# A convolution and two dense layers on one core: weights read in longer runs and with a stride, and another order of casts, loads and taps at the start

## The chip, the core and the metric

The kernel runs on one core of one Trainium2 chip. The metric is the device time of one execution, in microseconds (us); lower is better. The device time is some 1.7 us more than the span in the trace.

## The reference

x has 8 sequences of 4096 rows with 192 channels. A causal convolution of 7 taps runs along the sequence; the 192 channels are 8 heads of 24, and a head's taps are a softmax of 7 weights. Then each row goes through two dense layers, 192 to 2048 with a leaky ReLU and 2048 to 192.

```python
w = exp(weight - max); w = w / sum(w)                      # (8 heads, 7 taps)
out = np.einsum('hk,bskhg->bshg', w, x_unf)                # causal, 7 taps
h = out.reshape(B * S, D) @ w_in                           # 32768 x 192 @ 192 x 2048
g = np.maximum(0.01 * h, h)
return g @ w_out                                           # 2048 x 192
```

## The kernel before

Rows come in blocks of 512 for a pair of sequences. The first five blocks are worked in halves of 256 (ten half-blocks), the other 27 whole. VectorE does the taps of the convolution (`yt` from `xt`, three chunks of 64 channels for each of the two sequences, seven taps a chunk). TensorE does the hidden layer (`mm1`, from `yt` and `w_in` into PSUM tile `ph`), ScalarE evicts it with the leaky ReLU into `g`, and TensorE does the second layer (`po` from `g` and `w_out`) some blocks behind. Later blocks of x are loaded by casting DMAs that GpSimd issues (`load_x`) and transposed by DMA.

The first two blocks can't wait for that. They come in four "halves" q = 0 to 3, loaded in fp32, cast by an engine, transposed on TensorE and copied out of PSUM by VectorE:

```python
    def load_first(q, after=None):
        t = stage_pool.tile([128, 2, HS, D], FP32, name="x_nat")
        for e in range(2):
            ins = nc.sync.dma_start(out=t[:, e, :, :], in_=x[e, q * HT : (q + 1) * HT, :]...)
            # [cut: with `after`, the load waits for that instruction]

    def cast_first(q, e, copy):          # fp32 -> bf16, by VectorE or ScalarE
        copy(out=x_bf[q // 2][...], in_=x_nat[q][...])

    # [cut] transpose_first(q): 12 transposes on TensorE into PSUM; evac_first(q): two copies to xt
    make_identity(nc, ident)                                         # GpSimd
    nc.vector.tensor_add(ident2, ident[:, 0:CH], ident[:, CH:128])
    sel = const_pool.tile([H, NCH, 2, CH], BF16, name="sel")         # GpSimd: memset, two selects
    # [cut]
    w_in = const_pool.tile([128, NCH, F], BF16)                      # four quarters
    for fs in (slice(0, F // 2), slice(F // 2, F)):
        for e in range(2):
            nc.gpsimd.dma_start(out=w_in[e * CH : (e + 1) * CH, :, fs], in_=...)
    nc.gpsimd.dma_start(out=w_out, in_=moe_w_out.rearrange("(c p) d -> p c d", p=128))
    # [cut] softmax of the taps, beginning with nc.vector.tensor_reduce(out=nmax, ...)
```

In the loop over the groups, half-block 0 carries the special work (`u` counts the eight hidden steps):

```python
                act = mm1(grp, u)
                if i == 0 and u == 3:
                    for job in pe_ahead: job()       # one chunk of half 1's taps on TensorE
                if i == 0 and u in (0, 6):
                    load_first(2 + u // 6, act)
                if i == 1 and u in (2, 3):
                    cast_first(3, u - 2, nc.scalar.copy)
            # [cut]
            if i == 0 and j == 3:
                evac_y(nc.vector.tensor_scalar_mul)
                for e in range(2):
                    cast_first(2, e, nc.vector.tensor_copy)
                transpose_first(2)
                evac_first(2, nc.vector.tensor_copy, nc.vector.tensor_copy)
```

Of the kernel before, what the change touches and what calls it, by code (L numbers as in the profile page):

```python
# [14 lines left out]
def kernel(  # L15
# [28 lines left out]
    NHALF = 5  # L44
    NPEC = 2
# [59 lines left out]
    def load_first(q, after=None):  # L105
        t = stage_pool.tile([128, 2, HS, D], FP32, name="x_nat")
        for e in range(2):
            ins = nc.sync.dma_start(
                out=t[:, e, :, :],
                in_=x[e, q * HT : (q + 1) * HT, :].rearrange("(c p) d -> p c d", p=128),  # L110
            )
            if after is not None and e == 0:
                tc.add_manual_dep(
                    ins.ins, after.ins.name,
                    mybir.DependencyInfo(
                        mybir.DependencyClass.Sync, mybir.DependencyReason.DATA
                    ),
                    reason="leave the DMA engines to the weights",
                )
        x_nat[q] = t  # L120

    def cast_first(q, e, copy):
        if q % 2 == 0 and e == 0:
            x_bf[q // 2] = xb_pool.tile([128, NCH, SUB, 2, CH], BF16, name="x_bf")
        h = q % 2
        copy(  # L126
            out=x_bf[q // 2][:, :, h * HS : (h + 1) * HS, e, :],
            in_=x_nat[q][:, e, :, :].rearrange("p s (c k) -> p c s k", c=NCH),
        )
# [3 lines left out]
    def transpose_first(q):  # L133
        ts = [
            psum_o.tile([128, HS, NCH, CH], BF16, name=f"ptr{i}", tag="po") for i in range(2)
        ]
        for s in range(HS):
            for c in range(NCH):
                for i in range(2):
                    ps = slice(i * CH, (i + 1) * CH)  # L140
                    nc.tensor.transpose(  # L141
                        out=ts[i][:, s, c, :],
                        in_=x_bf[q // 2][ps, c, (q % 2) * HS + s, :, :].rearrange(
                            "p e k -> p (e k)"
                        ),
                        identity=ident[ps, ps],
                    )
        ptr[q] = ts

    def evac_first(q, *copies):  # L150
        dst = xt[0][:, :, HALO + q * HT : HALO + (q + 1) * HT].rearrange(
            "p c (s i k) -> p i s c k", s=HS, i=2
        )
        for i, t in enumerate(ptr.pop(q)):
            copies[i](out=dst[:, i], in_=t)  # L155
# [60 lines left out]
    nc.vector.memset(junk, 0.0)  # L216
    ident = const_pool.tile([128, 128], BF16)
# [4 lines left out]

    sel = const_pool.tile([H, NCH, 2, CH], BF16, name="sel")
    nc.gpsimd.memset(sel, 1.0)  # L224
    for sign, off in ((1, 0), (-1, GRP - 1)):
        nc.gpsimd.affine_select(  # L226
            out=sel, in_=sel, compare_op=mybir.AluOpType.is_ge, fill=0.0,
            base=off, channel_multiplier=-sign * GRP,
            pattern=[[sign * CH, NCH], [0, 2], [sign, CH]],
        )  # L230


    w_in = const_pool.tile([128, NCH, F], BF16)
    for fs in (slice(0, F // 2), slice(F // 2, F)):
        for e in range(2):
            nc.gpsimd.dma_start(  # L236
                out=w_in[e * CH : (e + 1) * CH, :, fs],
                in_=moe_w_in[:, fs].rearrange("(c p) f -> p c f", p=CH),
            )
    w_out = const_pool.tile([128, NFC, D], BF16)  # L240
    nc.gpsimd.dma_start(out=w_out, in_=moe_w_out.rearrange("(c p) d -> p c d", p=128))
# [4 lines left out]
    def warm(n):  # L246
        for _ in range(n):
            nc.tensor.matmul(  # L248
                out=wa[:, 0, 0:HT], lhsT=zero[:, 0:128], rhs=zero, start=True, stop=True
            )  # L250
# [20 lines left out]
    warm(9)  # L271
    wps = psum_h.tile([128, 2, ST], FP32, name="wps", tag="ph")
# [3 lines left out]
    def select(out, parts):  # L276
        for c in range(NCH):
            nc.tensor.matmul(
                out=out[:, c], lhsT=sel[:, c, :, :].rearrange("h e k -> h (e k)"),
                rhs=w9p[:, parts, :], start=True, stop=True,  # L280
            )
# [4 lines left out]
    warm(5)  # L286
# [44 lines left out]

    for n, job in enumerate(conv_jobs(groups[0], range(NPEC, NCH))):
        if n in (4, 5):
            cast_first(1, n - 4, nc.vector.tensor_copy)
        job()
    for c in range(NPEC):
        pe_jobs, evac_y = pe_conv_jobs(groups[0], c)
        for job in pe_jobs:
            job()
        evac_y(act_scale)  # L340
        if c == 0:
            warm(2)
    transpose_first(1)
    evac_first(1, nc.vector.tensor_copy, nc.vector.tensor_copy)


# [7 lines left out]
    SINGLE = LAST - 2  # L354

    def mm1(grp, u):
        blk, t0, T = grp
        y = yt[blk]
        nf = ST // T
        ph = psum_h.tile([128, 2, ST], FP32, name="ph", tag="ph")  # L360
        for i in range(nf):
            f = nf * u + i
            for c in range(NCH):
                for e in range(2):
                    ps = slice(e * CH, (e + 1) * CH)
                    nc.tensor.matmul(  # L366
                        out=ph[:, e, i * T : (i + 1) * T],
                        lhsT=w_in[ps, c, f * 128 : (f + 1) * 128],
                        rhs=y[ps, c, t0 : t0 + T],
                        start=(c == 0),  # L370
                        stop=(c == NCH - 1),
                    )
        act = nc.scalar.activation(  # L373
            out=g[blk][:, nf * u : nf * (u + 1), :, t0 : t0 + T],
            in_=ph.rearrange("p e (i t) -> p i e t", i=nf),
            func=mybir.ActivationFunctionType.Prelu, alpha=0.01,
        )
        return act
# [74 lines left out]
    pjunk = const_pool.tile([1, 1], BF16)  # L453
    slot, avail = 0, 0
    for i, grp in enumerate(groups):
# [11 lines left out]
        for j in range(steps):  # L467
            for u in range(2 * j, 2 * j + 2):
                act = mm1(grp, u)
                if i == 0 and u == 0:  # L470
                    pe_ahead, evac_y = pe_conv_jobs(groups[1], 0)
                    ahead = conv_jobs(groups[1], range(1, NCH))
                    per = len(ahead)
                if i == 0 and u == 3:
                    for job in pe_ahead:
                        job()
                if i == 0 and u in (0, 6):
                    load_first(2 + u // 6, act)
                if i == 1 and u in (2, 3):
                    cast_first(3, u - 2, nc.scalar.copy)  # L480
# [11 lines left out]
            if i == 0 and j == 3:  # L492
                evac_y(nc.vector.tensor_scalar_mul)
                for e in range(2):
                    cast_first(2, e, nc.vector.tensor_copy)
                transpose_first(2)
                evac_first(2, nc.vector.tensor_copy, nc.vector.tensor_copy)
            if i == 1 and j == 1:

                nc.gpsimd.tensor_copy(out=pjunk, in_=g[0][0:1, NFC - 1, 1, HT - 1 : HT])  # L500
                load_x(2)
# [4 lines left out]
            if i == 1 and j == 1:  # L506
                transpose_first(3)
# [44 lines left out]
```

## Time and profile before

| | before |
|---|---|
| time, median | 694.78 us (694.33 to 695.75, 3 runs); 694.98 with one more run |
| span of the profiled run | 693.2 us |
| TensorE, VectorE, ScalarE busy | 99%, 79%, 74% |
| first hidden step runs through from | 12.71 us |
| VectorE's copies of half 1 begin | 11.55 us |
| VectorE has finished block 5's convolution | 118.72 us |

TensorE's 99% says that little can be won at all: it is idle for 9.1 us of 693.2 (684.1 busy). Where a part of it can be won has to be read from the waits, engine by engine. The prediction below shows TensorE's. The following is VectorE's timeline of the kernel before: the softmax's first operation, then half 1's copies and what follows. Columns of all timelines below: start in us, duration in us, engine, source line, operation, output and input, how many in a row, and in brackets the idle time ahead with what ended it.

```profile
2.18 0.15 DVE L255 TENSOR_REDUCE nmax<-w 8x1 f32<-8x7 f32 x1 [0.57 <-DMA w<-in_weight_dram]
...
11.55 0.61 DVE L155 COPY xt<-ptr 128x384 bf16<-128x384 bf16 x2
...
18.85 0.48 DVE L205 TENSOR_SCALAR yt<-acc,rsum 128x256 bf16<-128x256 f32 x1
20.02 0.42 DVE L126 CAST x_bf<-x_nat 128x384 bf16<-128x384 f32 x1 [0.69 <-DMA x_nat<-in_x_dram]
21.25 0.43 DVE L126 CAST x_bf<-x_nat 128x384 bf16<-128x384 f32 x1 [0.81 <-DMA x_nat<-in_x_dram]
22.12 0.62 DVE L155 COPY xt<-ptr 128x384 bf16<-128x384 bf16 x2 [0.44 <-PE ptr L141]
...
26.10 0.58 DVE L174 TENSOR_SCALAR yt<-xt,wk 128x256 bf16<-128x256 bf16 x1
...
33.58 0.52 DVE L174 TENSOR_SCALAR yt<-xt,wk 128x256 bf16<-128x256 bf16 x1
...
37.14 0.28 DVE L174 TENSOR_SCALAR yt<-xt,wk 128x256 bf16<-128x256 bf16 x1
...
114.03 4.69 DVE L180 SCALAR_TENSOR_TENSOR yt<-xt,wk,yt 128x512 bf16<-128x512 bf16 x6
```

From 18.85 to 22.12 VectorE does no taps: 3.27 us of an eviction (of the chunk whose taps TensorE did), two casts and three waits. And the first tap of a chunk, always the same 128 x 256 operation, takes 0.28 us at 37.14 but 0.58 and 0.52 earlier.

### The profile page before, as it was taken

Reading aid. Unit: us, or ns where it says so; the run is one execution under the profiler, and the core shown is the slowest. Engines: PE = TensorE matmul, PEld = TensorE weight load, DVE = VectorE, ACT = ScalarE, POOL = GpSimd, SP = SyncE. Lnnn points to the kernel's source line nnn. Section 1 sums busy time; section 2 is a strip of 40 time slices with the busy share of each in tenths; the row PEclk is TensorE's granted clock in tenths of the full one; section 3 lists DMA queues with packets and bytes.
Section 4 is the critical chain, followed back from the end, with each engine's and each line's share of the span. In section 5 each row is a group of like instructions: output and inputs, shape, how many; then the busy total and the mean of one; then the engine's idle time right before and its main releaser. Section 6 shows DMA issues by size and latency. Waiting matters only on the chain.

```text
span 693.2 us, 26064 instructions
## 1 busy us (share of the span) xinstructions
PE 684.1 (99%) x11778; PEld 539.5 (78%) x11778; DVE 544.4 (79%) x1005; ACT 516.4 (74%) x577; POOL 139.6 (20%) x195
## 2 busy tenths in 40 slices
PE   7999999999999999999999999999999999999998
PEld 5899998677777777777777777777777777777777
DVE  7899998977878787878877888878777878787812
ACT  6788888977777777777777777777777777777771
POOL 3632201502222102222012222112222012000000
PEclk9999999999999999999999999999999999999999
DMA  9995636935565445565355664455655455222112
GB/s 167 124 102 81 87 67 82 90 73 70 72 88 79 72 77 76 74 82 84 69 81 74 78 82 78 78 70 75 86 82 78 74 75 66 70 60 59 48 36 70
DMA packets 184096, 54.39 MB, mean 78 GB/s; under 512 B 148400, under 2 KB 183216, under 8 KB 183984
## 3 DMA queue, kind: packets, MB, share of 16 engines
q0 software_dynamic: 97936, 14.17, 29.6%
q1 hardware_dynamic: 86048, 38.56, 22.7%
q8 instruction: 92, 1.51, 1.0%
q14 instruction: 20, 0.16, 0.1%
HBM read 29.88 MB, written 25.17 MB: 79 GB/s over the span
## 4 chain that ended last, share of the span: by engine, by line
PE 93%; DMA 3%; DVE 2%; ACT 1%; POOL 0%; issue 0%; SPq 0%; POOLq 0%; DVEq 0%
PE po L392 48%; PE ph L366 45%; DVE yt L180 2%; DMA w_in<-in_moe_w_in_dram 1%; DMA x_nat<-in_x_dram 1%; DMA xt<-x_bf 1%; ACT g L373 0%; POOL sel L226 0%; DVE yt L174 0%; ACT x_bf L126 0%; POOL w_in L236 0%; PE ptr L141 0%; DVE x_bf L126 0%; SPq L447 0%; POOL sel L224 0%
## 5 line engine op out<-in xcount | busy, mean ns | idle before, releaser
L373 ACT ACTIVATE g<-ph 128x1024 bf16<-128x1024 f32 x512 | 496.3, 1021 | 156.4 <-PE ph L366 156.1
L180 DVE SCALAR_TENSOR_TENSOR yt<-xt,wk,yt 128x512 bf16<-128x512 bf16 (+1 forms) x648 | 442.4, 683 | 17.6
L392 PEld LDWEIGHTS <-g 64*128 64x128 bf16 (+1 forms) x8064 | 352.3, 94 | 45.3 <-issue 0.2
L392 PE MATMUL po<-w_out,g 64*128 64x192 bf16 (+1 forms) x8064 | 382.7, 243 | 0.0
L366 PE MATMUL ph<-yt,w_in 64*128 64x512 bf16 (+1 forms) x3552 | 379.3, 347 | 3.1 <-DMA w_in<-in_moe_w_in_dram 1.2
L366 PEld LDWEIGHTS <-w_in 64*128 64x128 bf16 x3552 | 186.4, 94 | 98.6 <-issue 4.9
L77 POOL DMA_DIRECT2D x_bf<-in_x_dram x180 | 133.6, 772 | 422.4 <-DMA xt<-x_bf 420.0
L439 DVE COPY o_sb<-po 128x192 f32<-128x192 f32 x216 | 77.1, 358 | 121.1 <-PE po L392 115.3
L174 DVE TENSOR_SCALAR yt<-xt,wk 128x512 bf16<-128x512 bf16 (+1 forms) x108 | 38.0, 352 | 2.1 <-DMA xt<-x_bf 2.1
L439 ACT COPY o_sb<-po 128x192 f32<-128x192 f32 x40 | 12.8, 320 | 1.9
L248 PE MATMUL warm<-zero 128*128 128x256 bf16 x24 | 5.1, 367 | 1.1 <-DVE junk L216 1.1
L199 PE MATMUL acc<-xt,diag 64*64 64x256 bf16 x84 | 5.2, 270 | 0.5 <-DVE xt L155 0.5
L199 PEld LDWEIGHTS <-diag 64*64 64x64 bf16 x84 | 4.3, 106 | 1.3 <-DVE xt L155 0.8
L303 ACT ACTIVATE diag<-ident,whm 128x64 bf16<-128x64 bf16 x14 | 3.6, 335 | 1.9 <-DVE whm L289 1.9
L248 PEld LDWEIGHTS <-zero 128*128 128x128 bf16 x24 | 2.5, 124 | 2.2 <-DVE junk L216 1.1
L126 DVE CAST x_bf<-x_nat 128x384 bf16<-128x384 f32 x5 | 2.3, 453 | 1.5 <-DMA x_nat<-in_x_dram 1.5
L500 POOL COPY pjunk<-g 1x1 bf16<-1x1 bf16 x1 | 0.2, 178 | 16.1 <-ACT g L373 16.1
L141 PEld LDWEIGHTS <-x_bf 64*128 64x128 bf16 x48 | 1.0, 94 | 2.5 <-ACT x_bf L126 1.9
L141 PE MATMUL ptr<-ident,x_bf 64*128 64x64 bf16 x48 | 1.4, 191 | 1.4 <-ACT x_bf L126 0.9
L236 POOL DMA_DIRECT2D w_in<-in_moe_w_in_dram x4 | 2.6, 660 | 0.0
L155 DVE COPY xt<-ptr 128x384 bf16<-128x384 bf16 x7 | 2.2, 351 | 0.5 <-PE ptr L141 0.4
L253 ACT ACT_TABLE_LOAD x1 | 1.3, 1283 | 0.8 <-PEq L536 0.8
(35 smaller groups left out, 12.9 us busy)
## 6 DMA issues: line engine op xcount, KB each, us to landing
out_dram<-o_sb SPq DMA_DIRECT2D x123, 192.0 KB, 2.1
x_bf<-in_x_dram POOLq DMA_DIRECT2D x180, 64.0 KB, 3.3
x_nat<-in_x_dram SPq DMA_DIRECT2D x8, 192.0 KB, 3.9
w_in<-in_moe_w_in_dram POOLq DMA_DIRECT2D x4, 384.0 KB, 9.7
xt<-x_bf SPq DMA_TRANSPOSE x90, 2.6
out_dram<-o_sb SPq DMA_DIRECT2D x10, 96.0 KB, 1.6
w_out<-in_moe_w_out_dram POOLq DMA_DIRECT2D x1, 768.0 KB, 16.5
w<-in_weight_dram SPq DMA_DIRECT2D x1, 0.2 KB
```

Of the source, the lines that this page charges most:

```text
L77: nc.gpsimd.dma_start(out=t[:, c, :, e, :], in_=src[2 * rp + e, :, :, c * CH : (c + 1) * CH],)
L141: nc.tensor.transpose(out=ts[i][:, s, c, :], in_=x_bf[q // 2][ps, c, (q % 2) * HS + s, :, :].rearrange("p e k -> p (e k)"), identity=ident ...
L174: lambda s=src, d=dst, c=c: nc.vector.tensor_scalar_mul(d, s, wk[:, c, 0:1])
L180: lambda s=src, d=dst, c=c, k=k: nc.vector.scalar_tensor_tensor(out=d, in0=s, scalar=wk[:, c, k : k + 1], in1=d, op0=mybir.AluOpType.mult, ...
L199: lambda k=k, p=p, a=a, e=e, ps=ps: nc.tensor.matmul(out=acc[ps, :T], lhsT=diag[c][ps, p, k, :], rhs=xt[0][ps, c, a : a + T], start=(k == ...
L236: nc.gpsimd.dma_start(out=w_in[e * CH : (e + 1) * CH, :, fs], in_=moe_w_in[:, fs].rearrange("(c p) f -> p c f", p=CH),)
L248: nc.tensor.matmul(out=wa[:, 0, 0:HT], lhsT=zero[:, 0:128], rhs=zero, start=True, stop=True)
L303: nc.scalar.activation(out=diag[c][:, 1, k, :], in_=ident2, func=mybir.ActivationFunctionType.Copy, scale=whm[:, c, 1, k : k + 1],)
L366: nc.tensor.matmul(out=ph[:, e, i * T : (i + 1) * T], lhsT=w_in[ps, c, f * 128 : (f + 1) * 128], rhs=y[ps, c, t0 : t0 + T], start=(c == 0) ...
L373: act = nc.scalar.activation(out=g[blk][:, nf * u : nf * (u + 1), :, t0 : t0 + T], in_=ph.rearrange("p e (i t) -> p i e t", i=nf), func=my ...
L392: return nc.tensor.matmul(out=po[m], lhsT=g[b][ps, fc, e, s * 128 : (s + 1) * 128], rhs=w_out[ps, fc, :], start=start, stop=stop,)
L439: ins = copy(out=o_sb[:, n % 2, :], in_=po.pop(n))
```

## The change

The intent: start the hidden layer sooner and take waits and casts out of the first 30 us. Its parts, with the numbers that the prediction gives them: (1) a smaller selector and the first `w_in` issue ahead of the identity; (2) as a consequence, the identity later; (3) half 1's casts on ScalarE, its transposes behind the first hidden step, its x loaded by one DMA with two rows to a run; (4) halves 2 and 3 cast by GpSimd DMAs, queued without waiting; (5) half 1's TensorE taps in four parts, their result evicted by ScalarE and not by VectorE; (6) `w_out` in runs of four rows, for which `w_in`'s columns are read with a stride of 4; (7) ten more output tiles stored singly. Two things come with them and have no number of their own: the DMAs of block 2's x (`load_x(2)`) are queued without waiting too, and the fill-in matmuls (`warm`) at the start are a few more. The diff below is cut.

```diff
+    def load_first(q):                       # [cut to its core]
+        if q < 2:   # q == 1: one DMA, "e (p s) d -> p e (s d)"; q == 0 as before
+        elif q == 2:
+            for e in range(2):
+                nc.gpsimd.dma_start(out=x_rows[:, e], in_=rows[:, e])
+        else:
+            for c in range(NCH):
+                for e in range(2):
+                    nc.gpsimd.dma_start(out=x_half[q][:, c, :, e, :], in_=...)
@@ evac_first
-            "p c (s i k) -> p i s c k", s=HS, i=2
+            "p c (i k s) -> p i s c k" if q == RUNS else "p c (s i k) -> p i s c k",
@@ start
-    make_identity(nc, ident)
-    nc.vector.tensor_add(ident2, ident[:, 0:CH], ident[:, CH:128])
-    sel = const_pool.tile([H, NCH, 2, CH], BF16, name="sel")
+    sel = const_pool.tile([H, NCH, CH], BF16, name="sel")
     # [cut: sel's memset and selects]
+    load_w_in(0, 0)
+    make_identity(nc, ident)
+    nc.vector.tensor_add(ident2, ident[:, 0:CH], ident[:, CH:128])
+    load_w_in(0, 1)
+    for e in range(2):
+        load_w_in(1, e)
+    load_first(2)
-    nc.gpsimd.dma_start(out=w_out, in_=moe_w_out.rearrange("(c p) d -> p c d", p=128))
+    nc.gpsimd.dma_start(
+        out=w_out.rearrange("p (c i) d -> p c i d", i=RUN),      # RUN = 4
+        in_=moe_w_out.rearrange("(c p i) d -> p c i d", p=128, i=RUN),
+    )
+    load_first(3)
+    load_x(2)
@@ mm1
-                        lhsT=w_in[ps, c, f * 128 : (f + 1) * 128],
+                        lhsT=w_in[f * 2 // NFC][
+                            ps, c, f // RUN % 2 * RUN * 128 + f % RUN
+                            : (f // RUN % 2 + 1) * RUN * 128 : RUN
+                        ],
@@ loop
+                if i == 0 and u == 0:
+                    transpose_first(1)
+                    evac_first(1, nc.vector.tensor_copy, nc.vector.tensor_copy)
-                if i == 0 and u == 3:
-                    for job in pe_ahead:
+                if i == 0 and 2 <= u <= 5:
+                    n = len(pe_ahead) // 4
+                    for job in pe_ahead[(u - 2) * n : (u - 1) * n]:
                         job()
-                if i == 0 and u in (0, 6):
-                    load_first(2 + u // 6, act)
-                if i == 1 and u in (2, 3):
-                    cast_first(3, u - 2, nc.scalar.copy)
+                if i == 0 and u == 5:
+                    evac_y(act_scale)
+                if i == 0 and u == 6:
+                    transpose_first(2)
```

## The prediction

> **What bounds the kernel now.** I read the page first (busy shares), then the groups of instructions by shape in a steady window, the chain of waits in order of time, and the timelines of single engines in the two places where TensorE does not run full.
>
> ```profile
> PE 684.1 (99%) x11778; PEld 539.5 (78%) x11778; DVE 544.4 (79%) x1005; ACT 516.4 (74%) x577; POOL 139.6 (20%) x195
> PE   7999999999999999999999999999999999999998
> ...
> L366 PEld LDWEIGHTS <-w_in 64*128 64x128 bf16 x3552 | 186.4, 94 | 98.6 <-issue 4.9
> ...
> w_out<-in_moe_w_out_dram POOLq DMA_DIRECT2D x1, 768.0 KB, 16.5
> ```
>
> TensorE is busy 99% of the span, and the row by slices shows a gap only in the first slice and a little at the end. In the chain view, from 30 us on, one step of a half-block (24 matmuls of 256 columns, 32 of 192) takes 2.63 us and one of a full block (12 of 512, 32 of 192) 2.61. So only what happens before about 34 us, and at block changes, can be won. The head, in the chain:
>
> ```profile
> 3.65 9.02 DMA w_in<-in_moe_w_in_dram
> 12.66 0.04 issue
> 12.71 0.84 PE ph L366 x11
> ...
> 15.03 6.20 DMA x_nat<-in_x_dram
> 21.23 0.02 issue
> 21.25 0.44 DVE x_bf L126
> ...
> 27.97 0.41 ACT x_bf L126
> 28.38 0.05 issue
> 28.43 0.35 PE ptr L141 x12
> ```
>
> The first hidden layer starts at 12.71 when the second quarter of w_in has landed; half 2 of x is late (load asked for at 14.62, beside the weights), and half 3's casts stop TensorE until 28.43. Its steps before that are ACT-bound: eight Prelu evictions of about 0.97 us (four take 3.88) against 0.66 us of matmuls each.
>
> The second place is less visible. VectorE's timeline runs without a wait from 33.58 (end of group 2's convolution) to 118.72: seven groups of three chunks of 3.33 us, then a full block of 15.07, 85.1 us in all. TensorE reaches that block at 118.03 and waits for it:
>
> ```profile
> 118.03 1.78 PE L366 MATMUL ph<-yt,w_in 64*128 64x512 bf16 x12
> ...
> 120.78 0.35 DVE L174 TENSOR_SCALAR yt<-xt,wk 128x512 bf16<-128x512 bf16 x1 [2.06 <-DMA xt<-x_bf]
> ...
> 135.91 1.04 PE L366 MATMUL ph<-yt,w_in 64*128 64x512 bf16 x8 [0.34 <-DVE yt L180]
> ```
>
> A block start of 12 such matmuls takes 1.48 elsewhere, 1.78 here. From 119.20 to 135.78 ScalarE is then full (16 evictions and 4 output copies), and TensorE follows it; at 135.91 it waits 0.34 for VectorE. After 136.8 nothing waits. So up to 136 us **the chain that matters is VectorE's**, and an early TensorE is worth only what VectorE gains.
>
> **What the Trainium skill says.** "TensorE: Matmul & The Clock Gate", section "Back-to-back issue gap": a warm matmul of N columns takes N/2.4 + 2.5 ns. The two row halves run in pairs, so 12 pairs of 256 and 16 of 192 give 12 x 109.2 + 16 x 82.5 = 2.63 us, the step measured: the steady part has nothing to give. Same page, "Weight-path perf modes": fast weight load reads the columns "packed or strided", for 128 columns. "SBUF — State Buffer", in "Door 1: The DMA port swizzle": lines of 16 bytes, at least two hits in each for full speed, so bf16 may stride up to 8 elements. The change strides by 4, so both pages call it free; this trace has only packed loads (94 ns), so it does not show it. "VectorE: DVE Perf Modes", "What auto-detection actually checks": the 2x mode wants step 1 on 16-bit tensors; the new copies of half 1 write with step 2.
>
> **The change, part by part.**
>
> 1. w_in sooner. The chain has GpSimd at sel and ident until 2.95. The selector shrinks from 384 to 192 columns: memset 0.41, two selects 0.53 each; against the identity's 128 columns (0.20 and 0.29) I interpolate 0.26 and 0.35. The first w_in issue moves from 2.90 to about 1.9, the second (identity now between) from 3.65 to about 3.2. Data runs some 2.2 us after issue; I estimate the second landing at 11.9 instead of 12.67: minus 0.8.
>
> 2. What it delays. The identity is now built behind a DMA issue of 0.75, at about 3.2 instead of 1.38. The order of instructions shows VectorE taking its sum of the identity (waiting for GpSimd) before the softmax's first reduce, which ran at 2.18. So softmax, selection, diagonals, first transposes and first convolution shift by about 1.2 us. The second convolution eviction ended at 11.65, hence 12.9, with the six smaller selector matmuls 13.0. This overtakes the 11.9 of w_in: the first hidden step starts about where it does now (its first eviction was at 13.57; I get 13.6). **Part 1 is eaten by part 2.**
>
> 3. Half 1. Casts go from VectorE (2 x 0.42) to idle ScalarE; its transposes move behind the first hidden step. VectorE's copy of half 1 started at 11.55; now at 13.6 plus 0.5 (as 11.06 to 11.55 before) = 14.1: 2.5 later.
>
> 4. Halves 2 and 3 cast in the DMA, asked for without waiting. VectorE loses two casts (0.85), the eviction of the diagonal chunk (0.48, to ScalarE), and waits of 0.69, 0.81 and 0.44: 3.27 us. ScalarE loses half 3's casts (1.0), TensorE the wait at 28.43 (0.86). Half 2 costs 24 small transposes for 12, about 0.2 us beside ScalarE's evictions.
>
> 5. Half 1's taps in four parts: 0.4 us each between hidden steps, where ScalarE is the limit: the block of 1.72 at 16.32, with ScalarE's idle 1.40 after it, goes.
>
> 6. w_out in runs of four rows: 3 KB a descriptor for 768 B. Between 16 and 18 us the old form already moved 0.38 MB of bf16 in 2 us, as fast as w_in, so little is won; it landed at 22.0 and is first used at 23.4. Now behind half 2 in one queue, estimate 20.7, first use about 22.4. Hidden, no value.
>
> 7. Single-row stores for ten more tiles near the end: nothing waits for them; the last store after the last copy is the same. Zero.
>
> Sum for VectorE, from the copy of half 1 to the end of block 5's convolution: 107.17 us before (11.55 to 118.72). Minus 3.27, plus 0.2 for two strided copies (estimate from 0.35 to at most 0.45 each): 104.1. From 14.1: 118.2 instead of 118.72, **0.5 us won**. TensorE itself would be 1.3 us ahead there, so VectorE holds it. Block 5's evictions then end 0.5 earlier; the DMA transposes that VectorE awaited until 120.78 follow TensorE's pace and come over 1 us earlier, so the 0.34 at 135.91 goes too. Total about 0.85 us: 694.78 - 0.85 = 693.9.
>
> **Rivals.**
>
> A. The softmax delay is smaller than I think, or hidden. For: the fill-in matmuls before the selection were lengthened only by 128 columns, as if it moved by 0.1 us. Against: the order of instructions. Then half 1 begins at about 12.9 and the whole gain is near 2.0: 692.7. I give it a third.
>
> B. Strided weight loads become the limit. In half-blocks a pair of matmuls lasts 109 ns and needs two loads; if a strided load took the full 128 cycles unshared (estimate 2 x 107 ns), 480 pairs would lose about 0.1 us each: plus 50 us. In full blocks 216 ns hide it. The skill speaks against it: 5%.
>
> C. Casting DMAs of half 3 (128 B pieces) or the queued x blocks crowd out later transfers, or the fill-in hole at 3.4 to 4.5 us leaves TensorE's clock low in the first convolution: plus 1 to 2 us, time about 695.5. GpSimd's queue was idle until 22.8 and the pieces go in order, so 15%.
>
> D. A gain that TensorE keeps in full (its own waits of 3.5 us between 12.71 and 28.61): 691.2. VectorE's unbroken run to 118.72 speaks against it: 7%.
>
> **Range and chances.** Weighing 693.9 with A, C and D gives about 693.4. The runs before spread over 1.4 us, so eight in ten lie within 691.5 to 695.3. Two per cent is 13.9 us, more than all idle time before 34 us: faster 1%. Slower by over 2% needs B: 4%. Same: 95%.
>
> **What would show it.** Step 1: w_in's second landing near 11.9. Step 2: the softmax reduce near 3.4 instead of 2.18, and the first hidden eviction at 13.6 and not at 12.4. Step 3 and 4: VectorE's half-1 copy near 14.1, no waits of VectorE between it and 118, its block 5 finished near 118.2. Rival B: loads of w_in over 94 ns and a half-block step over 2.63. Step 6: w_out landed before TensorE asks. It would be wrong if VectorE still waited between 14 and 34 us, if steady steps changed, or if the head finished over 2 us earlier.

## The result, and the profile after

The changed kernel is correct and takes **694.84 us** in the median (693.86 to 695.57, 4 runs), the kernel before 694.98 (694.33 to 695.75, 4 runs on the same chip): ratio 0.9997, 95% interval 0.9979 to 1.0014, the same. A ratio here is the mean time of one kernel's fast runs over the mean of the other's of the same rounds, so it isn't quite the ratio of the medians quoted beside it.

The run that was profiled happens to be the fastest of the four: 693.86 us, span 692.2. That matters below.

The page of the changed kernel, in the rows that answer to those of the prediction, and two more of the DMA rows (size, then us from issue to landing):

```profile
PE 685.9 (99%) x11800; PEld 584.1 (84%) x11800; DVE 541.9 (78%) x1000; ACT 517.2 (75%) x578; POOL 144.6 (21%) x202
...
L402 PEld LDWEIGHTS <-w_in 64*128 64x128 bf16 x3552 | 227.3, 110 | 64.7 <-issue 4.1
...
w_in<-in_moe_w_in_dram POOLq DMA_DIRECT2D x4, 384.0 KB, 10.0
...
w_out<-in_moe_w_out_dram POOLq DMA_DIRECT2D x1, 768.0 KB, 14.6
```

A strided load of `w_in` takes 110 ns, a packed one took 94. Nothing waits for that: from 24.16 us on the steps are as long as before (2.63 us a half-block's, 2.61 a full block's), and from the second-layer piece after block 6's first hidden step to the last one of the loop it is 541.30 us (135.71 to 677.01) where it was 541.31. `w_out` lands 14.6 us after its issue for 16.5, at 21.1, and is first used at 24.16: hidden either way.

The timeline of the changed kernel in the first microseconds, all engines:

```profile
1.85 0.75 POOL L253 DMA_DIRECT2D w_in<-in_moe_w_in_dram  x1
...
2.90 0.29 POOL masks.py:199 TENSOR_SCALAR_AFFINE_SELECT ident<-ident 128x128 bf16<-128x128 bf16 x1
...
3.23 0.19 DVE L263 TENSOR_TENSOR ident<-ident 128x64 bf16<-128x64 bf16 x1 [2.15 <-POOL ident masks.py:199]
...
3.33 0.14 DVE L291 TENSOR_REDUCE nmax<-w 8x1 f32<-8x7 f32 x1
...
4.33 0.33 PE L316 MATMUL wps<-w9p,sel 8*64 8x16 bf16 x6 [1.00 <-DVE w9p L304]
```

`w_in` is asked for 1.05 us sooner. But VectorE waits 2.15 us for the identity with the softmax behind it, so the softmax's reduce runs at 3.33 (before: 2.18), and TensorE waits a microsecond for the softmax. Then VectorE's timeline, which answers to the one shown of before:

```profile
14.20 1.06 DVE L176 COPY xt<-ptr 128x384 bf16<-128x384 bf16 x2 [2.11 <-PE ptr L156]
15.29 0.29 DVE L195 TENSOR_SCALAR yt<-xt,wk 128x256 bf16<-128x256 bf16 x1
...
21.95 0.61 DVE L176 COPY xt<-ptr 128x384 bf16<-128x384 bf16 x2
22.59 0.29 DVE L195 TENSOR_SCALAR yt<-xt,wk 128x256 bf16<-128x256 bf16 x1
...
112.97 0.35 DVE L195 TENSOR_SCALAR yt<-xt,wk 128x512 bf16<-128x512 bf16 x1
113.35 4.69 DVE L201 SCALAR_TENSOR_TENSOR yt<-xt,wk,yt 128x512 bf16<-128x512 bf16 x6
119.42 0.36 DVE L195 TENSOR_SCALAR yt<-xt,wk 128x512 bf16<-128x512 bf16 x1 [1.38 <-DMA xt<-x_bf]
```

Half 1 begins 2.65 us later than before; from there VectorE has no wait at all and ends block 5 at 118.04 (113.35 + 4.69), 0.68 sooner than before. In TensorE's timeline of the changed kernel block 5 begins at 117.71 and runs without a wait, and the wait of 0.34 that the prediction shows at 135.91 is gone:

```profile
117.71 1.49 PE L402 MATMUL ph<-yt,w_in 64*128 64x512 bf16 x12
...
134.41 1.50 PE L402 MATMUL ph<-yt,w_in 64*128 64x512 bf16 x12
```

So this one run came within 0.2 us of what the prediction's sum said (118.2 for VectorE, 693.9 for the time). The other three runs took 694.55 to 695.57. The question for the experiments was not why the mechanism failed, but why the median did not show it.

### The profile page after: what moved, and what is told of

Read it like the earlier page. It is cut to its first block, busy times and chain, and to the rows that moved or that the text cites. A ratio compares the mean times of both kernels' runs of the same rounds, so it can differ in the third digit from the quotient of the medians.

```text
span 692.2 us, 26117 instructions
## 1 busy us (share of the span) xinstructions
PE 685.9 (99%) x11800; PEld 584.1 (84%) x11800; DVE 541.9 (78%) x1000; ACT 517.2 (75%) x578; POOL 144.6 (21%) x202
## 4 chain that ended last, share of the span: by engine, by line
PE 97%; ACT 2%; POOL 0%; DVE 0%; issue 0%; POOLq 0%
PE po L431 48%; PE ph L402 47%; ACT g L412 1%; PE acc L220 1%; PE warm L283 1%; POOL w_in L253 0%; POOL sel L242 0%; PE ptr L156 0%; PE wps L316 0%; ACT yt L367 0%; ACT w L295 0%; DVE o_sb L478 0%; PE ptr L163 0%; POOL ident masks.py:199 0%; POOL sel L240 0%
## 5 line engine op out<-in xcount | busy, mean ns | idle before, releaser
L431 PEld LDWEIGHTS <-g 64*128 64x128 bf16 (+1 forms) x8064 | 360.6, 94 | 34.0 <-issue 0.2
L431 PE MATMUL po<-w_out,g 64*128 64x192 bf16 (+1 forms) x8064 | 387.3, 243 | 0.0
L402 PE MATMUL ph<-yt,w_in 64*128 64x512 bf16 (+1 forms) x3552 | 384.1, 347 | 1.2 <-ACT g L412 0.5
L402 PEld LDWEIGHTS <-w_in 64*128 64x128 bf16 x3552 | 227.3, 110 | 64.7 <-issue 4.1
L283 PE MATMUL warm<-zero 128*128 128x256 bf16 (+1 forms) x28 | 6.4, 399 | 1.1 <-DVE junk L237 1.1
L134 POOL DMA_DIRECT2D x_half<-in_x_dram x6 | 4.3, 716 | 6.5 <-DMA w_in<-in_moe_w_in_dram 6.5
L367 ACT ACTIVATE yt<-acc,rsum 128x256 bf16<-128x256 f32 x3 | 1.4, 466 | 0.8 <-PE acc L220 0.8
(37 smaller groups left out, 14.7 us busy)
## 6 DMA issues: line engine op xcount, KB each, us to landing
w_out<-in_moe_w_out_dram POOLq DMA_DIRECT2D x1, 768.0 KB, 14.6
```

The source lines that it names most:

```text
L134: nc.gpsimd.dma_start(out=x_half[q][:, c, :, e, :], in_=rows[:, e, :, c * CH : (c + 1) * CH],)
L283: nc.tensor.matmul(out=wa[:, 0, 0:cols], lhsT=zero[:, 0:128], rhs=zero[:, 0:cols], start=True, stop=True,)
L402: nc.tensor.matmul(out=ph[:, e, i * T : (i + 1) * T], lhsT=w_in[f * 2 // NFC][ps, c, f // RUN % 2 * RUN * 128 + f % RUN : (f // RUN % 2 + ...
L431: return nc.tensor.matmul(out=po[m], lhsT=g[b][ps, fc, e, s * 128 : (s + 1) * 128], rhs=w_out[ps, fc, :], start=start, stop=stop,)
```

## The experiments

Theory: VectorE's run from half 1's copies to the end of block 5's convolution sets the time. Rivals: TensorE's own waits in the head; the strided loads; a transfer; chance. Eleven kernels were built and run, two of them repeats, with executions of the kernel before, which took 695.07 (11 executions), 695.05 (9) and 694.74 us (11).

### 1. The changed kernel again

No edit.

> The changed kernel unaltered, for a tighter interval. The two traces differ by 1.0 us of span (692.2 against 693.2). Theory (the trace's gain is real and small): ratio to before 0.9980 to 0.9993, that is 0.5 to 1.4 us faster. Rival (the profiled run was a lucky one; nothing gained): ratio 0.9993 to 1.0007.

694.66 us (693.64 to 696.20, 6 runs), ratio 0.9994 [0.998, 1.0008]. Again the same as before. The profiled run was a slower one (695.50, span 693.8), and it shows what the fast one hid. VectorE's timeline first, then TensorE's and GpSimd's, of this run:

```profile
22.77 0.38 DVE L195 TENSOR_SCALAR yt<-xt,wk 128x256 bf16<-128x256 bf16 x1
...
26.19 0.67 DVE L195 TENSOR_SCALAR yt<-xt,wk 128x256 bf16<-128x256 bf16 x1
...
29.89 0.66 DVE L195 TENSOR_SCALAR yt<-xt,wk 128x256 bf16<-128x256 bf16 x1
```

```profile
119.80 1.06 PE L402 MATMUL ph<-yt,w_in 64*128 64x512 bf16 x8 [1.40 <-DVE yt L201]
```

```profile
20.87 12.60 POOL L79 DMA_DIRECT2D x_bf<-in_x_dram  x17 [1.84 <-DMA w_out<-in_moe_w_out_dram]
43.65 4.45 POOL L79 DMA_DIRECT2D x_bf<-in_x_dram  x6 [10.19 <-DMA xt<-x_bf]
```

Half 1's copies began at 14.14, like in the other run. But the first taps of six chunks took 0.38 to 0.67 us for 0.28, together 1.8 us, VectorE ended block 5 at 119.75, and TensorE waited 1.40 for it. Every stretched tap lies inside one of GpSimd's runs of DMA issues (the first of the six at 18.56, inside an issue from 18.25 to 19.03). What follows: the spread of the runs is in VectorE's chain, and GpSimd is the suspect (experiments 9 and 10).

### 2. The softmax ahead of VectorE's sum of the identity, twice

```diff
-    nc.vector.tensor_add(ident2, ident[:, 0:CH], ident[:, CH:128])     # ahead of the softmax
 ...
     nc.vector.tensor_sub(w9p[:, 2], w9r, w9p[:, 1])
+    nc.vector.tensor_add(ident2, ident[:, 0:CH], ident[:, CH:128])     # behind it
```

> The changed kernel, only VectorE's sum of the two identity halves moved behind the softmax instructions in its order. Theory (the softmax was delayed 1.2 us by that sum): the softmax reduce starts near 2.2 us instead of 3.33, VectorE's copy of half 1 starts 0.6 to 1.1 us sooner than 14.20 (w_in's second quarter, landing near 12.5, becomes the limit), block 5's convolution ends near 117.2 instead of 118.04, span about 0.5 to 0.7 us shorter than the changed kernel's 692.2. Rival (half 1's own load, 8.4 us from issue to landing, or w_in holds the start): copy of half 1 still at 14.0 to 14.3, span unchanged within 0.2.

693.26 us (692.44 to 694.19, 6 runs), ratio **0.9975** [0.9963, 0.9987]. VectorE's reduce is back at 2.17, half 1's copies begin at 12.45 instead of 14.20 (1.75 us sooner, where 0.6 to 1.1 was expected), and block 5's convolution ends at 116.69. Now `w_in` is what the first hidden step waits for, as TensorE's timeline of this run shows:

```profile
11.41 0.84 PE L402 MATMUL ph<-yt,w_in 64*128 64x256 bf16 x11 [0.25 <-DMA w_in<-in_moe_w_in_dram]
```

The second run of the same kernel, on another chip:

> The kernel of e2_sum_late, unaltered, a second time. If what it won was real (half 1's copies 1.75 us sooner, so VectorE's run to block 5 begins and ends sooner), its time is again 1.3 to 2.0 us under the kernel before, ratio 0.9971 to 0.9981. If it was luck with stretched first taps (the rival), the ratio is 0.999 or more and the trace shows VectorE at block 5 as late as 118.

694.22 us (692.86 to 695.02, 6 runs), ratio 0.9991 [0.9977, 1.0004]: outside the expected 0.9971 to 0.9981, so that expectation missed. The trace says why in two numbers. TensorE waited longer for the same quarter of `w_in`,

```profile
12.59 0.84 PE L402 MATMUL ph<-yt,w_in 64*128 64x256 bf16 x11 [1.19 <-DMA w_in<-in_moe_w_in_dram]
```

so half 1 began at 13.62; and 1.8 us of stretched taps fell on this run where the first had 0.4. The part that the edit rules, the softmax, is as early in both. Together the two put the cost of the delayed softmax at about 1 us (an estimate: the mean of the two ratios is 0.9983, where the changed kernel had 0.9997 and 0.9994, so 0.8 to 1.0 us). The second interval includes no gain at all, and the edit hands the start over to `w_in`, whose landing moves by a microsecond from run to run. It is the best version found, but no interval was taken against the changed kernel.

### 3. Part 4 alone: the kernel before with only halves 2 and 3 cast in the DMA

```diff
+    load_cast(2)                     # two casting DMAs ahead of w_out
     nc.gpsimd.dma_start(out=w_out, ...)
+    load_cast(3)                     # six behind it
 ...
-                if i == 0 and u in (0, 6):
-                    load_first(2 + u // 6, act)
-                if i == 1 and u in (2, 3):
-                    cast_first(3, u - 2, nc.scalar.copy)
+                if i == 0 and u == 5:
+                    transpose_first(2)
 ...
-                for e in range(2):
-                    cast_first(2, e, nc.vector.tensor_copy)
-                transpose_first(2)
```

> The kernel before with only halves 2 and 3 of x cast in the DMA (and half 2's transposes moved before the seventh hidden step); selector, w_in, w_out, half 1, taps as before. Theory (this part carries the gain; part 3 of the prediction gave some of it back): half 1's copy on VectorE stays at 11.55, VectorE ends block 5's convolution near 116.4 instead of 118.72, TensorE reaches that block near 117.0 instead of 118.03, span 691.3 to 691.9, as good as or better than the whole change. Rival (the gain needs the earlier w_in and the smaller selector): span at 693 within 0.3.

694.76 us (694.46 to 695.47, 5 runs), ratio 0.9996 [0.9984, 1.0008]. TensorE is 1.26 us ahead at block 5 (116.77 for 118.03) and waits there: `1.20 <-DVE`, until VectorE is ready at 118.53. Half 1's copies began at 12.35, VectorE waited 1.08 once, and 1.5 us of stretched taps took the rest. The expected time was missed; what is confirmed is that TensorE's lead alone is worth nothing (the prediction's rival D).

The copies were expected at 11.55, for up to there the edit changes only what GpSimd issues. What differs is TensorE's convolution of half 0, first in the kernel before, then in this run:

```profile
7.43 1.72 PE L199 MATMUL acc<-xt,diag 64*64 64x256 bf16 x28 [0.53 <-DVE xt L155]
```

```profile
7.51 2.55 PE L224 MATMUL acc<-xt,diag 64*64 64x256 bf16 x28
```

The same 28 matmuls take 0.83 us longer, and the copies come 0.80 later. "All traces in one sum" takes this up.

### 4. The weights packed as before

```diff
-                        lhsT=w_in[f * 2 // NFC][ps, c, <start> : <stop> : RUN],
+                        lhsT=w_in[f * 2 // NFC][ps, c, f % (NFC // 2) * 128 : (f % (NFC // 2) + 1) * 128],
 ...
-        out=w_out.rearrange("p (c i) d -> p c i d", i=RUN),
-        in_=moe_w_out.rearrange("(c p i) d -> p c i d", p=128, i=RUN),
+        out=w_out, in_=moe_w_out.rearrange("(c p) d -> p c d", p=128),
```

> The changed kernel with w_out loaded row by row again and w_in's columns read packed. Theory (the strided weight load costs 110 ns instead of 94 but lies under the matmuls; the runs of four rows make w_out land earlier where nobody waits): weight loads 94 ns, half-block step 2.63 and full-block step 2.61 us as now, w_out lands 0.5 to 1.5 us later than 21.1, span 692.2 within 0.3. Rival (stride costs TensorE in half blocks): step shorter, span over 1 us shorter. Rival (w_out's early landing is worth something): span over 0.5 us longer, TensorE waiting for w_out.

694.10 us (693.83 to 695.52, 6 runs), ratio 0.9990 [0.9977, 1.0003]. The loads are back at 94 ns, steps are 2.63 and 2.61 us as with the stride, and `w_out` lands 14.7 us after its issue, against 14.6 with runs of four rows. Part 6 does nothing to the time: neither its stride nor its longer runs are felt.

### 5. Half 1 early again

Experiment 2's order, and half 1 with plain loads, VectorE's casts behind block 0's convolution, and transposes ahead of the first hidden step.

```diff
-    RUNS = 1
+    RUNS = -1                                       # half 1 loaded as half 0 is
 ...
+    for e in range(2):
+        cast_first(1, e, nc.vector.tensor_copy)     # and no longer on ScalarE
 ...
+    transpose_first(1)                              # ahead of the first hidden step
+    evac_first(1, nc.vector.tensor_copy, nc.vector.tensor_copy)
```

> The changed kernel with the softmax first (as in the run before this) and half 1 as in the kernel before: two plain loads, casts on VectorE behind block 0's convolution, transposes ahead of the first hidden step, copies with step 1. Theory (VectorE's chain to block 5 sets the end, TensorE close behind): copies of half 1 start 0.3 to 0.8 us before the 12.45 of e2_sum_late and take 0.35 us each instead of 0.53; VectorE is ready for block 5 about 1 us earlier than e2_sum_late's 116.7 and no longer waited for, TensorE gains only its 0.16 us wait plus what half 1's transposes save, span 690.2 to 690.8 in a run without stretched first taps, ratio to before 0.9960 to 0.9980. Rival (VectorE still sets all): span 1 us under e2_sum_late's 690.7.

694.21 us (694.03 to 695.44, 5 runs), ratio 0.9990 [0.9978, 1.0003]. Half 1's two copies take 0.62 us together, as in the kernel before, and not 1.06: it is the two-row run, whose copies write with a step of 2, that slows them. They begin at 12.48, no earlier than in experiment 2, because VectorE's casts wait for x until 11.04; and VectorE then waits 0.88 for the transposes of half 2. The expectation missed: no gain over experiment 2.

### 6. More work for VectorE

Six copies of 128 x 384 fp32 in half-block 4, which nobody reads.

```diff
+            if i == 4 and j == 0:
+                for _ in range(6):
+                    nc.vector.tensor_copy(out=vdummy, in_=x_nat[0][:, 0, :, :])
```

> The changed kernel with six more copies of 384 fp32 elements on VectorE (estimate 1.6 us in all) in group 4, whose result nobody reads. Theory (VectorE's unbroken run up to block 5 sets the time): block 5's convolution ends 1.6 us later than 118.04, TensorE waits over 1 us there, and the span grows by 1.2 to 1.7 us. Rival (TensorE at 99% busy sets the time, VectorE has slack at 78%): span unchanged within the spread of 0.8.

698.19 us (696.65 to 699.40, 4 runs), ratio 1.0041 [1.0024, 1.0057]. VectorE's timeline of this run, then TensorE's:

```profile
54.33 2.33 DVE L529 COPY vdummy<-x_nat 128x384 f32<-128x384 f32 x6
```

```profile
66.68 1.29 PE L402 MATMUL ph<-yt,w_in 64*128 64x256 bf16 x20 [1.21 <-DVE yt L201]
...
121.91 1.06 PE L402 MATMUL ph<-yt,w_in 64*128 64x512 bf16 x8 [2.23 <-DVE yt L201]
```

The copies lengthen VectorE's run by 2.25 us, and all of it arrives at the end: the time rises by about 3 us (695.05 to 698.19; the ratio's interval is 1.7 to 4.0 us, so 2.25 is inside it). VectorE is busy only 78% of the span, and until 118 us it is the bound.

### 7. One first tap of each half-block on ScalarE

On top of experiment 5, to keep that tap away from GpSimd's issues.

```diff
+        tap = ahead.pop(2 * K) if 1 <= i < 2 * NHALF - 1 else None
 ...
+            if tap is not None and j == 1:
+                tap(act_scale)
```

> e7_early_half1 with one of the three first taps of groups 2 to 9 moved from VectorE to ScalarE (0.3 us each off VectorE, eight times; ScalarE has 0.33 us idle per half-block step). Theory (the spread between runs comes from first taps stretched while GpSimd issues DMAs, on a VectorE chain without slack): VectorE reaches block 5 over 2 us before TensorE, so stretched taps no longer reach TensorE: no wait of TensorE for VectorE in the trace, spread of runs under 1 us instead of 1.7 to 2.6, median 0.3 to 1 us under e7_early_half1. Rival (the spread comes from the loads at the start): spread as before. Risk: ScalarE becomes late in half blocks and TensorE waits for its evictions.

694.58 us (693.75 to 696.57, 5 runs), ratio 0.9985 [0.9971, 0.9999]. The spread did not shrink, so the expectation missed. VectorE now waits 0.8 us at a time for ScalarE's tap (2.3 us in three waits from 80 to 104 us). The profiled run was the slowest (696.57), and it shows a second source of spread, which experiment 3 showed too: TensorE's first 28 matmuls of half 0's convolution took 3.19 us, against 1.72 in eight of the thirteen traces, and half 1's copies began at 14.88. In this trace the second load of half 0 landed at 6.58 us, against 4.3 in most others, TensorE stood idle for 0.87 us before the transposes that need it, and its matmuls ran at half their later rate until 13.3 us.

### 8. Half 1's taps in one piece

```diff
-                if i == 0 and 2 <= u <= 5:
-                    n = len(pe_ahead) // 4
-                    for job in pe_ahead[(u - 2) * n : (u - 1) * n]:
+                if i == 0 and u == 3:
+                    for job in pe_ahead:
                         job()
```

> The changed kernel with half 1's diagonal taps as one block again. Theory (each part costs TensorE two changes of tile shape, and what it wins from ScalarE's idle time it loses there; VectorE sets the end anyway): the second layer's first matmul starts within 0.4 us of the 24.16 of the changed kernel, block 5 as VectorE allows. Rival (the split keeps ScalarE fed): it starts over 0.6 us later.

One execution (state unknown), 694.54 us, span 692.8. The second layer begins at 23.70 and not at 24.16; half 1's copies began 0.5 earlier in this run too (13.70), so the four parts neither win nor lose anything that this run could show. VectorE ends block 5 at 118.77 and TensorE waits 0.95 for it.

### 9 and 10. GpSimd's issues more than doubled, and the same DMAs issued by SyncE

In each of the four steps of half-blocks 2 to 8, two more small DMAs, which nobody reads; in the one kernel GpSimd issues them, in the other SyncE.

```diff
+            if 2 <= i <= 8:
+                nc.gpsimd.tensor_copy(out=pjunk, in_=g[blk][0:1, 4 * j, 1, t0 : t0 + 1])
+                for _ in range(2):
+                    nc.gpsimd.dma_start(                  # control: nc.sync.dma_start
+                        out=idle_dst[:, n_idle % 8],
+                        in_=x[0, 0:ST, 0:16].rearrange("(s p) d -> p s d", p=128),
+                    )
```

> The changed kernel with 56 idle DMA issues of GpSimd between 34 and 104 us (two per step of the half-blocks, each of 512 small pieces, their data read by nobody). Theory: VectorE's first taps of a chunk are stretched because GpSimd is writing the descriptors of a DMA meanwhile. In the trace of the changed kernel GpSimd issues for 18 us of these 70; here for some 50 to 60. So most of the 24 first taps should take 0.4 to 0.7 us for 0.28, VectorE reach the end of block 5's convolution 4 to 8 us later than 118.0, TensorE wait there 3 to 7 us, and the time rise to 697.5 to 702. Rival (the stretch comes from traffic of DMAs, or is noise): the stretches stay as they were, the time within 0.7 of the changed kernel's, or as in e11_issue_sync.

> The control for e10_issue_gpsimd: the same 56 DMAs, the same small pieces (not cast), asked for by SyncE and not by GpSimd. Theory (GpSimd's own issue stretches VectorE's first taps): the first taps stay at 0.28 to 0.32 us on average as in the changed kernel, and the time within 1 us of it (693.9 to 695.9). Rival (traffic of DMAs stretches them): the same stretches and the same loss as in e10_issue_gpsimd.

With GpSimd 695.85 us (695.60 to 696.44, 4 runs), ratio 1.0016 [1.0002, 1.0030]; with SyncE 696.20 (694.97 to 697.25, 4), ratio 1.0021 [1.0002, 1.0039]. The first expectation missed. So did the control's in the time, but its first taps stayed short, as it said (0.31 us on average from 20 us on). GpSimd issued for 60 us between 20 and 104 us, for 28 in the changed kernel, yet VectorE ended block 5 at 118.91 with 1.33 us of stretched taps, far from the 4 to 8 us expected. And both lost about a microsecond in another place: block 6's DMA transposes released VectorE at 121.34 and 121.15 and not at 119.42, and the GpSimd version has a wait of 0.79 at 136.71 again. Whether the extra DMAs delay those transposes is not shown: each kernel has one trace, and the kernel before (120.78) and experiment 7 (121.30) have them as late without any extra DMA.

The two traces still settle the question when the taps are counted one by one. All 13 traces, the first taps of 256 columns from 20 to 104 us:

| first taps (128 x 256) | number | over 0.33 us |
|---|---|---|
| while GpSimd issues a DMA, GpSimd version | 19 | 5 |
| while GpSimd issues a DMA, the other twelve traces | 102 | 41 |
| while it doesn't, all thirteen | 183 | 0 |

No tap outside an issue is ever stretched, with SyncE's 56 extra DMAs in flight either: it is GpSimd's issue, not the traffic. Inside, the place decides. One issue takes some 0.75 us. Placed within their issue, the taps of all thirteen traces fall apart like this: of 24 that begin in its first 0.17 us none is held; of 41 that begin 0.20 to 0.48 us into it every one is (0.33 to 0.67 us for 0.28); of 39 that begin later none takes more than 0.34. (At 0.17 to 0.20 some are held and some are not.) Every held tap ends 0.02 to 0.06 us after its issue has ended: the tap of 0.67 us above begins 0.21 into an issue, the one of 0.38 begins 0.44 into it. Put by the end of the tap, all three groups are one: a tap that would be done in 0.28 us before some 0.46 of the issue have passed goes through, one that would end after that waits for the end of the issue, and one that would end after the issue anyway loses nothing. So a tap loses at most 0.47 us and often nothing, and doubling the issues only adds chances. An estimate from these figures: a tap that begins anywhere in an issue has a chance of about 0.30/0.76 to begin where it is held, and loses some 0.2 us there; 19 taps then lose 1.5 us. Measured were 1.0 us on these taps (the rest of the 1.33 is on taps of 512 columns). The expectation had let nearly every tap be held.

### All traces in one sum

For each profiled run: A, when VectorE begins half 1's copies; S, the time of first taps over 0.28 us (0.35 for 512 columns) from there on; R, when VectorE ends block 5's convolution; and F, when TensorE comes to its full rate: until then a matmul of 256 columns (or a pair of them that run side by side) starts every 0.21 us, from then on every 0.11. (The profiler's granted clock reads 1.00 before F as well.) All in us.

| run | F | A | S | R | R - A - S | span | span - R |
|---|---|---|---|---|---|---|---|
| before | 5.9 or sooner | 11.55 | 0.67 | 118.72 | 106.50 | 693.2 | 574.5 |
| changed | 9.1 | 14.20 | 0.05 | 118.04 | 103.79 | 692.2 | 574.2 |
| changed, again (1) | 9.1 | 14.14 | 1.82 | 119.75 | 103.79 | 693.8 | 574.1 |
| softmax first (2) | 5.5 | 12.45 | 0.42 | 116.69 | 103.82 | 690.7 | 574.0 |
| softmax first, again (2) | 7.1 | 13.62 | 1.82 | 119.23 | 103.79 | 693.3 | 574.1 |
| casting DMAs alone (3) | 9.3 | 12.35 | 1.50 | 118.53 | 104.68 | 692.8 | 574.3 |
| packed weights (4) | 8.3 | 13.78 | 1.03 | 118.60 | 103.79 | 692.6 | 574.0 |
| half 1 early (5) | 5.7 | 12.48 | 1.13 | 117.94 | 104.33 | 692.4 | 574.5 |
| VectorE copies (6) | 7.9 | 14.06 | 1.76 | 121.86 | 106.04 | 695.9 | 574.0 |
| tap on ScalarE (7) | 13.3 | 14.88 | 0.18 | 120.33 | 105.27 | 694.9 | 574.6 |
| taps in one piece (8) | 8.1 | 13.70 | 1.28 | 118.77 | 103.79 | 692.8 | 574.0 |
| issues by GpSimd (9) | 8.3 | 13.81 | 1.33 | 118.91 | 103.77 | 694.0 | 575.1 |
| issues by SyncE (10) | 10.1 | 14.66 | 0.80 | 119.27 | 103.81 | 694.1 | 574.8 |

In the eight traces with the changed kernel's VectorE program and nothing added to it, R - A - S is the same to 0.05 us, and but for the two traces with extra DMAs the span is R plus 574.0 to 574.6. The time of a run is its A plus its S plus a constant. A moves between 13.7 and 14.7 for one order of instructions, S between 0 and 1.8.

A goes with F. In the seven traces whose start is the changed kernel's (changed, 1, 4, 6, 8, 9, 10) the later F, the later A, from 13.70 to 14.66; only experiment 6 stands out, and there TensorE waited for `w_in`, which landed at 12.98, the latest of all. With the start of the kernel before, F at 5.9 or sooner gave 11.55 and F at 9.3 gave 12.35 (experiment 3). So a run's time hangs on three draws: when TensorE comes to its full rate, when `w_in` lands, and how many taps an issue holds. What sets F is not shown.

This also gives an estimate of what the change is worth. Without stretched taps the kernel before would end block 5 at 118.05 (118.72 - 0.67) and the changed one at 117.99: nothing won. What is left is the wait of 0.34 at 135.91. That is some 0.4 us, 0.06%; the two ratios are 0.9997 and 0.9994. But the kernel before has one trace, with an early F. With the A of 12.35 that its start had in experiment 3 it would end at 118.85, and the changed kernel with its own A of 13.70 to 14.66 at 117.5 to 118.5. One pair of traces can't settle half a microsecond here; the ratios, whose intervals include 1, are what is measured.

## Why the prediction was right, and which terms were off

"The same" was right, the median fell inside the range, and the mechanism (VectorE's run to block 5) holds. That the profiled run met the sum of 693.9 us so closely is luck: the sum saved 0.36 us too much, carried 0.67 us of chance stretches over from the before trace, and met a run that happened to have next to none. Point by point:

- **What bounds the kernel**: right. VectorE's run to block 5 sets the time (experiment 6: 2.25 us more of it, some 3 us more time; experiment 3: TensorE 1.26 us ahead, nothing won). Rival D fell with that. The steady step of 2.63 us does follow the formula that the prediction cites; the page gives it for an isolated matmul and says that a stream can differ; this one did not.
- **Part 1, `w_in` sooner**: the issues were at 1.85 and 3.14, as put ("about 1.9", "about 3.2"). The landing of the second quarter was estimated at 11.9. It landed at 12.54 in the changed kernel's profile, at 11.82 in experiment 1, and at 11.37 and 12.54 in the two of experiment 2. It was asked for 0.51 us sooner (3.14 for 3.65; the first quarter 1.05). But with the issue times of the kernel before it landed at 12.66 in that kernel's profile and at 11.36 in experiment 3. So no gain from asking sooner is shown; the landing moves by more than that by itself.
- **Part 2, what it delays**: right. The reduce ran at 3.33 (put at 3.4); the second convolution eviction ended at 13.22 (12.9 to 13.0), the first hidden eviction began at 14.05, 0.45 later than put (part of it is TensorE's half rate up to 9.1 us). **Rival A**, that the delay is smaller or hidden, fell: it came in full. Experiment 2 puts its cost at about 1 us.
- **Part 3**: copies at 14.20, put at 14.1. But the two strided copies take 1.06 us for 0.62, 0.44 more; the term was 0.2. "VectorE: DVE Perf Modes", section "What auto-detection actually checks", gives the condition that they miss (step 1 on 16-bit tensors), and experiment 5 with plain rows has 0.62.
- **Part 4**: right to the hundredth. The copies of half 2 follow the last tap directly at 21.95, so the 3.27 us are gone.
- **Part 5**: "the block of 1.72, with ScalarE's idle 1.40 after it, goes" came true only in part. It became four rounds of 1.33 us, between which ScalarE idles 0.31 us three times, 0.93 in place of 1.40. Nothing in the time hung on it: the sum has no term for it, and experiment 8, without the part, shows no loss.
- **Part 6**: hidden, as put. The stride of 4 that the prediction read as free in the skill is not free for the load itself, 110 ns for 94. **Rival B** fell all the same: its 2 x 107 ns for a pair was an assumption, and no step got longer. **Part 7**: zero, as put.
- **Rival C**: no queued transfer held up the changed kernel's profile (no wait for one between 14.20 and 118.04). Its other half, a low rate of TensorE at the start, came true in part: in all seven traces with the changed start the full rate comes only at 7.9 to 10.1 us, behind the hole (a wait of 1.00 ahead of 4.33), where the two traces of experiment 2, without the hole, have 5.5 and 7.1. In the changed kernel's profile it costs about 0.5 us (A is 14.20, where experiment 8 has 13.70), not the 1 to 2 that were put. That the hole causes it is not shown: experiments 3 and 7 have no hole either, and 9.3 and 13.3.
- **The sum for VectorE, "0.5 us won"**: this is the mis-sized step. It took the 107.17 us of the before trace as a fixed length, though 0.67 us of it were first taps stretched by chance, and it had no such term for the kernel after. The fixed lengths are 106.50 and 103.79: 2.71 us less, for which half 1 begins 2.65 later. The prediction had 3.07 less (3.27 - 0.2). Of the missing 0.36, 0.24 is the strided copies; 0.11 is the copies of half 3, which stood within a chunk before (0.54 us) and stand between two chunks now (0.65).
- **The 693.4**: it lies 1.4 us under the median of 694.84. Of that, 0.5 us is the weight given to rivals A and D, 0.36 the saving that was put too high, 0.1 half 1's later copies (14.20 for 14.1), and 0.2 the kernel before itself, which came out at 694.98 and not at the 694.78 that the sum starts from. The remaining 0.3 is less than the runs differ by chance: S alone is 1.2 us on average over the seven traces with the changed VectorE order (changed, 1, 2 twice, 4, 6, 8: 8.18 / 7), where the profiled run had 0.05.

The mechanism behind the missing term stands in the skill: "SBUF — State Buffer", section "Who interferes with whom", says that VectorE and GpSimd share a pair of ports, that VectorE's copy, cast and tensor_scalar in their fast two-port modes take that pair for a whole instruction, and that the other engine then blocks fully. The traces agree in kind: the first tap is a tensor_scalar and is held; the six others of a chunk (scalar_tensor_tensor) take 485 ns on average in all thirteen traces, inside an issue as outside. That the tap runs in such a mode is the page's reading: no run here shows the mode, only its 0.28 us for the 0.485 of the others at the same size. The prediction cited another section of that page and did not look for this one, though its own trace had taps of 0.58, 0.52 and 0.40 us.

## What to carry to other kernels

Before taking a stretch of one engine's timeline as a fixed length, compare each operation in it with its own shortest instance: what is longer in one place than in another is a term of its own, and may be chance. An early load bought with a later small operation on another engine wins only if the later one is not on the path; the order of instructions on each engine tells that beforehand, and one sum of 0.19 us moved behind the softmax measured as more, in the mean of its two calls, than the whole change (though the second call alone doesn't show it). And when a change is worth less than the spread of the runs, look for the two or three numbers per trace that make up the spread, and don't take one trace's start for the kernel's: the fastest run of four is not the typical one.

## What the Trainium skill lacked or had wrong

- "SBUF — State Buffer", "Who interferes with whom": the lock is told as a whole instruction against a whole instruction. For VectorE against a DMA issue of GpSimd the runs show that it depends on the moment: issues of some 0.75 us, taps begun 0.20 to 0.48 us into one held until 0.02 to 0.06 us after its end, taps in its first 0.17 and in its last quarter microsecond not held; 46 of 121 taps that met an issue were held, by up to 0.47 us, and 0 of 183 that met none.
- "TensorE: Matmul & The Clock Gate", "Weight-path perf modes", names packed and strided columns in one breath and gives no separate time for strided ones. With a stride of 4 in bf16 a load of 128 columns took 110 ns, packed 94 (experiment 4 has both back to back). No matmul waited for it here.
- I found no page that tells how much the landing of a weight DMA moves from run to run: the same quarter of `w_in` with the same issue order landed at 11.4 and at 12.5 us (experiment 2, on two chips), and that moved the whole span.
